# Two token chunks take the first inner half in two parts, with four attention jobs in flight

## The chip, the cores and the metric

The kernel runs on one core of one Trainium2 chip. The metric is the device time of one execution in microseconds (us); lower is better. The kernel before takes 661.24 us in the median of three runs (659.5 to 663.07). Engine names are those of the profile: PE (TensorE matmuls), DVE (VectorE), ACT (ScalarE), POOL (GpSimd), SP (the engine that issues the DMAs).

## The reference

Three layers follow each other: an attention, a gated two-layer network, and a mixture of four experts. Weights, queries, keys and values arrive in float32, except that the network's weights `w_in` and `w_out` are float64 in memory.

```
q, k, v: 2 batches x 8 heads x 576 tokens x 64
q_d, k_d, v_d = means over groups of 4 tokens                # 144 tokens
out_d   = softmax(q_d k_d^T / 8) v_d, repeated 4 times
scores  = q k^T / 8, kept where |i - j| < 4
x = out_d + softmax(scores) v                                # 1152 tokens x 512
h = x @ w_in (512 x 2048);  g = h * sigmoid(h);  x = g @ w_out (2048 x 512)
p = domain_probs / sum
out = sum over 4 experts of p[:, e] * (relu(x @ w1[e]) @ w2[e])   # 512 -> 1024 -> 512
```

## The kernel before, in words

**Attention.** A job is one batch, one pair of heads (four pairs) and one token part (256 or 320 tokens): 16 jobs, numbered in the order batch, part, pair. Jobs 0 to 3 give the 256 tokens of chunk 0, jobs 4 to 7 the 320 of chunk 1, and so on. Each job has named steps, which the orders below use with the job's number: S (local scores on PE), x (maximum and subtraction on DVE), e (exponential on ACT), q, k, p (sums of four queries or keys), D (scores of the averaged tokens on PE), n and d (their maximum on DVE, exponential on ACT), u and r (sums, reciprocals and scaling on DVE), g (scaling on ACT), T (transposes on PE), a (copies on ACT), v (sums of four values on POOL), V (values on PE), o, f (the two attentions added), h and l (x split into a high and a low part, on ACT and DVE). A tail per batch (tp, tD, nt, dt, ...) does the averaged queries of the last 64 tokens.

**Network.** Every float32 product is done as three products of split operands (`mm3`, L563 to L567): high x high, high x low, low x high. `w_in` and `w_out` come as eight units of four pieces (512 KB each): units 0 and 1 are the first inner half (1024 of 2048) of `w_in`, units 2 and 3 that half of `w_out`, units 4 to 7 the second half. A piece s is loaded and split: A (one or two ACT passes over the raw float64), B (one DVE pass, for the pieces in `LOW_ON_DVE`), C (DVE, L230), w (high part), L (low part, POOL, L240). `G c_f_k` is one row block of the first product (chunk c, inner block f of 8, quarter k of the 512 inputs), `H c_d_f` one block of the second (output block d of 4, inner block f). After the G of a block come th (tanh on ACT), gf (DVE, L586), gh (ACT) and gl (DVE, L592). `M k` is G of chunk 0 for the first three inner blocks, quarter k, taken while attention runs; it needs only job k's part of x and piece k.

**Order in time.** For each inner half, the chunks follow one another: all eight G blocks of a chunk, then its H, so chunk 0 needs all 16 pieces of units 0 to 3 before chunk 1 begins. PSUM has three `mm` tiles for these products, two `s` tiles for scores. Work is issued with a priority by tick; `WRITTEN` (L861) then fixes, for each engine apart, the order of the named steps of jobs 0 to 7, chunk 0 and the G of chunk 1. Jobs 8 to 15 are placed by ticks, beside chunk 1's H and chunk 2's G. From chunk 2's H on, and in the experts (L794), there is no attention left.

```
    for hf in range(2):
        u0 = 4 * hf
        for ci, (o, n) in enumerate(CHUNKS[hf]):
            for ft in range(8):
                    g1_step(u0, ft, o, n)
            for db in range(4):
                    g2_step(u0 + 2, hf, [db], o, n)
```

Of the kernel before, what the change touches and what calls it, by code (L numbers as in the profile page):

```python
# [57 lines left out]
LOW_ON_DVE = (0, 3, 9, 13)  # L58
WHI_ON_DVE = (3, 4)
# [4 lines left out]
def attention_moe_kernel(ctx, tc, kqa, kqb, qtl, va, vb, w64, w1d, w2d, dpr, out):  # L64
# [136 lines left out]

    def split_piece():
        u, j, t = loaded.popleft()
        i = 4 * u + j
# [3 lines left out]
        if i < 10 or 11 < i < 15 or i > 15:  # L208
            load_piece()

    def split_raw(u, j, t):
        if j == 0:
            unit[u] = slot(u)
        h, l = unit[u]
        if u < 8:
            c = slice(j * 512, (j + 1) * 512)
# [10 lines left out]
            else:  # L227
                low = mark(f"A{4 * u + j}", ACT.activation(out=v[:, :, 0], in_=top, func=ACTF.Copy, scale=2.0 ** -13,  # L228
# [4 lines left out]
            if 4 * u + j == 16:  # L233
                for a, b in ((first, "gh0_7"), (low, "gh0_7"), (i, "gl0_7")):
                    follow(a, steps[b][-1], "written order")
            if 4 * u + j in WHI_ON_DVE:
                mark(f"w{4 * u + j}", DVE.tensor_copy(out=h[:, c], in_=d))
            else:
                mark(f"w{4 * u + j}", ACT.activation(out=h[:, c], in_=d, func=ACTF.Copy))  # L239
            mark(f"L{4 * u + j}", POOL.tensor_tensor(out=l[:, c], in0=d, in1=h[:, c].bitcast(F32), op=ALU.subtract))  # L240
        else:
            c = slice(j * 1024, (j + 1) * 1024)
# [6 lines left out]
    a2 = actx.enter_context(tc.tile_pool(name="a2", bufs=2))  # L249
    a4 = actx.enter_context(tc.tile_pool(name="a4", bufs=4))  # L250
# [9 lines left out]

    def constants():
        POOL.memset(mask, 0.0)
        for h in range(2):
            m = mask[64 * h:64 * h + 64]
            POOL.affine_select(out=m, in_=m, pattern=[[0, 6], [1, WIN]], compare_op=ALU.is_ge,
                               fill=NEG, base=0, channel_multiplier=-1)
            POOL.affine_select(out=m, in_=m, pattern=[[0, 6], [-1, WIN]], compare_op=ALU.is_ge,
                               fill=NEG, base=6, channel_multiplier=1)
        POOL.memset(mask[:, 0, 0:3], NEG)
        POOL.memset(mask[:, 5, WIN - 3:WIN], NEG)  # L270
        make_identity(nc, ident)
# [13 lines left out]
    def load_kq(j):  # L285
        kw = S + 6 if j.c == 0 else CT[1] + 6
        if j.i == 3:
            j.kq = acc[:, 0:kw + j.n]
# [4 lines left out]
        i = load(f"kq{j.i}", j.kq, (kqa, kqb)[j.c][j.b, j.hp])  # L293
        if j.i == 3:
            first_kq.append(i)
        elif j.i in (4, 5):
            follow(i, first_kq[0], "first jobs")
        elif j.i in (8, 9):
            follow(i, piece_load[j.i + 5], "weights")
# [12 lines left out]
    def load_vg(j):  # L312
        if j.c == 0:
# [4 lines left out]
            i = load(f"vg{j.i}", j.vg, va[j.b, j.hp, :, 0:1024])  # L318
            if j.i == 8:
                follow(i, piece_load[13], "weights")  # L320

    def load_tail(l):
        t = ac.tile([128, 256, 4], F32, tag="vg", name="qt")
        l.t = t[:, 0:64]
        i = load("qt" if l.b == 0 else "qt1", l.t, qtl[l.b].rearrange('p (n r) -> p n r', r=4))
        if l.b == 0:
            follow(i, first_kq[0], "first jobs")
# [23 lines left out]
    def pool_kq_first(j):  # L351
        kd[j.b, j.hp] = a4.tile([128, SD], F32, tag="kd", name="kd")
        k4 = j.k[:, 3:3 + S].rearrange("p (n r) -> p n r", r=4)
        mark(f"k{j.i}", DVE.tensor_reduce(out=kd[j.b, j.hp], in_=k4, axis=AX.X, op=ALU.add))
        j.qd = qbd[j.hp % 2]
        q4 = j.q[:, 0:256].rearrange("p (n r) -> p n r", r=4)
        for h in range(2):
            p = slice(64 * h, 64 * h + 64)
            mark(f"q{j.i}", DVE.tensor_reduce(out=j.qd[p, h], in_=q4[p], axis=AX.X, op=ALU.add))
# [55 lines left out]
    def down_scores(j):  # L415
        i = PE.matmul(out=j.ps[:, 352:352 + SD], lhsT=j.qd.rearrange("p a b -> p (a b)"), rhs=kd[j.b, j.hp],
# [19 lines left out]
    def norm(j):  # L436
# [4 lines left out]
        if nb:  # L441
            j.sm = a2.tile([128, nb, WIN], F32, tag="sm", name="sm")
# [69 lines left out]
    def plan_jobs():  # L512
        k = 0
        for b in range(NB):
            for c in range(2):
                for hp in range(HP):
# [46 lines left out]
    def mm3(ps, pairs, first, last):  # L563
# [534 lines left out]
```

## Time and profile before

| what | value |
|---|---|
| median of three runs | 661.24 us (659.5 to 663.07) |
| span of the profiled execution, first to last instruction | 657.7 us |
| median less that span (what lies around it, and the spread of runs) | 3.5 us |
| PE busy in the span | 630.2 us (96%) |
| DVE, ACT, POOL busy | 418.8, 327.6, 245.3 us |

The profile states no other time for the profiled execution than its span. Busy times of one engine are joined where instructions overlap; a single instruction's duration overlaps its neighbour's by about 0.1 us on DVE and ACT, so sums below use the distance between starts. The idle time of PE lies almost wholly in the first 76 us and in the last 18 us; in between PE is busy without a break.

### The profile page before, as it was taken

What the parts mean: (1) busy time and instruction counts of PE and PEld (TensorE: products, weight loads), DVE (VectorE), ACT (ScalarE), POOL (GpSimd) and SP (SyncE); (2) the same over time, 40 slices, a digit from 0 to 9 for tenths busy, and PEclk for the clock granted to TensorE, in tenths of its full rate; (3) what the DMA queues carried; (4) which work ended last, traced back from release to release, by engine and by line L of the source; (5) the groups of instructions that cost most, each with busy time, mean ns of one, the idle gap of its engine ahead of it and who ended that gap; (6) DMA issues with size and microseconds to landing.
All of it is one profiled execution on the core that took longest, in us unless ns stands there. A gap on an engine that the chain in (4) does not pass through costs nothing.

```text
span 657.7 us, 13693 instructions
## 1 busy us (share of the span) xinstructions
PE 630.2 (96%) x5484; PEld 616.3 (94%) x5484; DVE 418.8 (64%) x862; ACT 327.6 (50%) x744; POOL 245.3 (37%) x345
## 2 busy tenths in 40 slices
PE   4788999999999999999999999999999999999995
PEld 3677899999999999999999999999999999999995
DVE  6698465655545545766558956668954679755434
ACT  4789654568845434363345633346533356433321
POOL 5554651114510001653456322645522564333210
PEclk9899999999999999999999999999999999999998
DMA  9986512106612200240004310014300020000001
GB/s 260 328 283 181 170 54 73 26 5 196 191 59 65 65 1 1 65 161 1 1 1 129 97 33 2 1 34 129 97 1 1 1 65 1 1 33 33 1 33 50
DMA packets 16928, 48.17 MB, mean 73 GB/s; under 512 B 2976, under 2 KB 4256, under 8 KB 16864
## 3 DMA queue, kind: packets, MB, share of 16 engines
q1 hardware_dynamic: 16864, 47.29, 23.4%
q8 instruction: 43, 0.70, 0.5%
q14 instruction: 21, 0.17, 0.1%
HBM read 44.93 MB, written 2.36 MB: 72 GB/s over the span
## 4 chain that ended last, share of the span: by engine, by line
PE 79%; DMA 11%; DVE 3%; ACT 3%; POOL 2%; issue 1%; SPq 0%; ACTq 0%; POOLq 0%; DVEq 0%
PE mm L565 50%; PE p L794 26%; DMA stg<-in_w_dram 4%; DMA vg<-in_va_dram 2%; DMA acc<-in_kqa_dram 2%; DMA acc<-in_w_dram 2%; DMA qt<-in_qtl_dram 1%; DVE dec L230 1%; ACT stg L228 1%; PE t L455 1%; POOL vg L330 1%; ACT dec L222 1%; DMA kq<-in_kqa_dram 1%; PE o L487 1%; DVE acc L822 1%
## 5 line engine op out<-in xcount | busy, mean ns | idle before, releaser
L565 PE MATMUL mm<-xh,wbuf 128*128 128x256 f32 (+2 forms) x1280 | 263.8, 293 | 2.6 <-DVE gf L586 2.3
L565 PEld LDWEIGHTS mm<-xh,wbuf 128*128 128x128 f32 x1280 | 208.2, 188 | 4.1 <-DVE gf L586 3.3
L565 PE MATMUL mm<-xl,wbuf 128*128 128x256 f32 (+2 forms) x640 | 186.9, 292 | 0.0
L776 POOL TENSOR_TENSOR r<-r 128x128 f32<-128x128 f32 x160 | 95.3, 608 | 177.6 <-ACT r L770 136.2
L779 DVE TENSOR_TENSOR h<-r,h 128x384 fp32r<-128x384 f32 (+1 forms) x128 | 91.9, 719 | 64.5 <-ACT h L778 64.2
L778 ACT ACTIVATE h<-r 128x384 fp32r<-128x384 f32 (+1 forms) x128 | 73.7, 578 | 93.7 <-POOL r L776 54.2
L565 PEld LDWEIGHTS mm<-xl,wbuf 128*128 128x128 f32 x640 | 120.3, 188 | 0.0
L565 PE MATMUL mm<-gh,wbuf 128*128 128x256 f32 (+2 forms) x512 | 103.3, 295 | 0.3 <-DVE gf L586 0.2
L794 PE MATMUL p<-wext,h 128*128 128x256 f32 x672 | 89.4, 276 | 0.0
L565 PEld LDWEIGHTS mm<-gh,wbuf 128*128 128x128 f32 x512 | 82.2, 188 | 1.2 <-ACT acc L635 0.4
L794 PE MATMUL p<-wbuf,h 128*128 128x256 f32 x672 | 82.7, 276 | 0.0
L794 PEld LDWEIGHTS p<-wext,h 128*128 128x128 f32 x672 | 82.4, 188 | 0.0
L794 PEld LDWEIGHTS p<-wbuf,h 128*128 128x128 f32 x672 | 79.4, 188 | 0.0
L565 PE MATMUL mm<-gl,wbuf 128*128 128x256 f32 (+2 forms) x256 | 74.1, 292 | 0.0
L776 DVE TENSOR_TENSOR r<-r 128x128 f32<-128x128 f32 x96 | 39.3, 409 | 35.6 <-ACT r L770 31.2
L770 ACT ACTIVATE r<-mm 128x512 f32<-128x512 f32 x48 | 28.6, 597 | 65.3 <-PE mm L565 65.0
L565 PEld LDWEIGHTS mm<-gl,wbuf 128*128 128x128 f32 x256 | 48.1, 188 | 0.1
L592 DVE TENSOR_TENSOR gl<-gf,gh 128x256 fp32r<-128x256 f32 (+2 forms) x64 | 34.6, 543 | 17.9 <-ACT gh L591 17.5
L240 POOL TENSOR_TENSOR wbuf<-dec,wbuf 128x512 fp32r<-128x512 f32 x24 | 32.0, 1350 | 33.8 <-ACT wbuf L239 32.3
L591 ACT ACTIVATE gh<-gf 128x256 fp32r<-128x256 f32 (+2 forms) x64 | 28.1, 442 | 21.6 <-DVE gf L586 20.7
L822 DVE SCALAR_TENSOR_TENSOR acc<-p,pr,acc 128x256 f32<-128x256 f32 (+1 forms) x63 | 36.1, 604 | 3.5 <-PE p L794 3.0
L586 DVE SCALAR_TENSOR_TENSOR gf<-th,mm 128x256 f32<-128x256 f32 (+2 forms) x64 | 28.5, 451 | 14.9 <-ACT th L585 13.9
(138 smaller groups left out, 895.8 us busy)
## 6 DMA issues: line engine op xcount, KB each, us to landing
stg<-in_w_dram SPq DMA_DIRECT2D x25, 512.0 KB
kst<-in_w2d_dram SPq DMA_DIRECT2D x16, 512.0 KB
kst<-in_w1d_dram SPq DMA_DIRECT2D x12, 512.0 KB
acc<-in_w_dram SPq DMA_DIRECT2D x7, 512.0 KB
kq<-in_kqb_dram SPq DMA_DIRECT2D x8, 323.0 KB
kq<-in_kqa_dram SPq DMA_DIRECT2D x6, 419.0 KB
stg<-in_w1d_dram SPq DMA_DIRECT2D x4, 512.0 KB
vw<-in_vb_dram SPq DMA_DIRECT2D x8, 180.0 KB
```

The lines of the kernel that those rows point to most:

```text
L222: first = ACT.activation(out=d, in_=v[:, :, 1].bitcast(F32), func=ACTF.Prelu, scale=2.0 ** -112, alpha=2.0 ** 32)
L240: mark(f"L{4 * u + j}", POOL.tensor_tensor(out=l[:, c], in0=d, in1=h[:, c].bitcast(F32), op=ALU.subtract))
L565: ins = [PE.matmul(out=ps, lhsT=l, rhs=r, start=(first and i == 0), stop=(last and i == n - 1)) for i, (l, r) in enumerate(pairs)]
L586: mark(f"gf{c}_{ft}", DVE.scalar_tensor_tensor(out=gf[:, 0:n], in0=th[:, 0:n], scalar=1.0, in1=ps[:, 0:n], op0=ALU.add, op1=ALU.mult))
L591: latest[ACT] = mark(f"gh{c}_{ft}", ACT.activation(out=gh[ft][:, 0:n], in_=gf[:, 0:n], func=ACTF.Copy))
L592: latest[DVE] = mark(f"gl{c}_{ft}", DVE.tensor_tensor(out=gl[ft][:, 0:n], in0=gf[:, 0:n], in1=gh[ft][:, 0:n].bitcast(F32), op=ALU.subtract))
L770: ACT.activation(out=r[:, 0:4].rearrange("p s t -> p (s t)"), in_=ps[:, 0:512], func=ACTF.Relu)
L776: latest[eng] = eng.tensor_tensor(out=r[:, o], in0=r[:, a], in1=r[:, b], op=op)
L778: ACT.activation(out=h, in_=r[:, part], func=ACTF.Copy)
L779: latest[DVE] = DVE.tensor_tensor(out=l, in0=r[:, part], in1=h.bitcast(F32), op=ALU.subtract)
L794: ins = [PE.matmul(out=ps, lhsT=x, rhs=y, start=(opens and k == 0 and i == 0), stop=(k == 3 and i == n - 1), skip_group_check=True) for i, ...
L822: DVE.scalar_tensor_tensor(out=o, in0=ps, scalar=p, in1=o, op0=ALU.mult, op1=ALU.add)
```

## The change

Chunks 0 and 1 take the first inner half in two parts: `quarter(ci, p, ...)` does four G blocks and the half of H that belongs to them, for chunk 0 part 0, chunk 1 part 0, chunk 0 part 1, chunk 1 part 1. Part 0 needs only units 0 and 2, part 1 units 1 and 3, and the pieces are loaded and split in the order of units 0, 2, 1, 3. The sum of the first part waits in `acc`, and the second is added to it by a DVE instruction. `M` covers all four blocks of chunk 0 part 0, in two PSUM tiles with two blocks each. Jobs 0 to 3 have their scores open at once: jobs 2 and 3 in two of the `mm` tiles. Their averaged keys move from DVE to POOL; jobs 0 and 1 don't use them for D but sum over the raw keys on PE. The written order now covers all 16 jobs and chunks 0 and 1 whole, up to the first product of chunk 2. The second inner half and the experts are as before.

```diff
         u0 = 4 * hf
+        if hf == 0:
+            for p in range(2):
+                for ci in range(2):
+                    main_at[1] = ci
+                    quarter(ci, p, *CHUNKS[0][ci])
...
+            if hf == 0 and ci < 2:
+                continue
...
+    def quarter(ci, p, o, n):
+        c = slice(o, o + n)
+        g = [4 * ci + i for i in range(4)]
+        two = n == 256
+        for i in range(4):
+            next_step()
+            ft = 4 * p + i
+            if (ci, p) == (0, 0):
+                g1_evac(half(hold[i // 2], i % 2), ft, n, g[i])
+            else:
+                g1_step(0, ft, o, n, g[i])
+            attn_tick()
+        flush()
+        if two:
+            b = [mm_tile() for _ in range(2)]
+            groups = [[(d, half(b[d // 2], d % 2)) for d in range(4)]]
+        else:
+            groups = [[(d, mm_tile()) for d in ds] for ds in ((0, 1, 2), (3,))]
...
+                        m = PE.matmul(out=ps[:, 0:n], lhsT=a[:, s], rhs=y, start=(not z and i == 0 and x == 0),
+                                      stop=(i == 3 and x == 2), skip_group_check=True)
...
+                if p == 0:
+                    i = ACT.activation(out=ya, in_=ps[:, 0:n], func=ACTF.Copy, scale=0.5)
+                else:
+                    i = DVE.scalar_tensor_tensor(out=ya, in0=ps[:, 0:n], scalar=0.5, in1=ya, op0=ALU.mult, op1=ALU.add)
...
-LOW_ON_DVE = (0, 3, 9, 13)
-WHI_ON_DVE = (3, 4)
+LOW_ON_DVE = (0, 1, 2, 3)
+WHI_ON_DVE = ()
+RAW_D = (0, 1)
...
+    ORDER = (0, 2, 1, 3)
+    firsts = deque((u, j) for u in ORDER for j in range(4))
...
-    def pool_kq_first(j):
...
-        mark(f"k{j.i}", DVE.tensor_reduce(out=kd[j.b, j.hp], in_=k4, axis=AX.X, op=ALU.add))
...
+    def pool_q_first(j):
+        j.qp = a4.tile([128, 64], F32, tag="qp", name="qp")
+        mark(f"q{j.i}", DVE.tensor_reduce(out=j.qp, in_=j.q.rearrange("p (n r) -> p n r", r=4), axis=AX.X, op=ALU.add))
...
+    def pool_k_first(j):
...
+        mark(f"k{j.i}", fold(k4), padd(kd[j.b, j.hp], k4[:, :, 0], k4[:, :, 1]))
...
-        j.ps = s_p.tile([128, 512], F32, tag="s", name="s")
+        j.ps = mm_tile() if j.i in (2, 3) else s_p.tile([128, 512], F32, tag="s", name="s")
...
+        if j.i in RAW_D:
+            k4 = j.k[:, 3:3 + S].rearrange("p (n r) -> p n r", r=4)
+            first = [None, None]
+            for r in range(4):
+                for h in range(2):
+                    p = slice(64 * h, 64 * h + 64)
+                    i = PE.matmul(out=j.ps[p, 352:352 + SD], lhsT=j.qp[p], rhs=k4[p, :, r], start=(r == 0), stop=(r == 3),
+                                  skip_group_check=True)
...
     WRITTEN = (
...
-        """S0 S1 D0 D1 S2 T0 S3 T1 V0 D2 D3 V1 M0 T2 V2 M1 T3 S4 V3 M2 D4 S5 M3 tD G0_3_0 G0_3_1 D5 G0_3_2 G0_3_3
...
+        """S0 S2 S1 D0 S3 D1 D2 T0 S4 D3 V0 T1 S5 D4 V1 T2 M0 D5 T3 V2 tD M1 S6 V3 T4 M2 D6 S7 tT M3 V4 T5 D7 S8 H0_0_0
+        H0_1_0 H0_2_0 H0_3_0 T6 V5 H0_2_1 H0_0_1 H0_1_1 D8 S9 G1_0_0 H0_3_1 H0_2_2 H0_3_2 H0_0_2 H0_1_2 T7 V6 G1_0_1 S10
...
```

On PE, at the end of chunk 0's early blocks: rows of before from the last three matmuls of M3 on. `o` and `t` are PSUM tiles of V and T, `s` of S and D.

```order
L565 MATMUL mm<-xh,wbuf 128x256 x2
L565 MATMUL mm<-xl,wbuf 128x256
L565 MATMUL mm<-xh,wbuf 128x256
L424 MATMUL s<-kd,qdl 32x144 x4
L565 MATMUL mm<-xh,wbuf 128x256
L565 MATMUL mm<-xl,wbuf 128x256
L565 MATMUL mm<-xh,wbuf 128x256 x2
L565 MATMUL mm<-xl,wbuf 128x256
L565 MATMUL mm<-xh,wbuf 128x256
L416 MATMUL s<-kd,qbd_103 128x144
```

After M3 come more G blocks of chunk 0, and a D. The same place of the changed kernel, where L981 is M and L696 is H:

```order
L981 MATMUL mm<-xl,wbuf 128x256
L981 MATMUL mm<-xh,wbuf 128x256
L514 MATMUL o<-atd_618,vd 64x80 x4
L518 MATMUL o<-at,vw 64x64 x10
L486 MATMUL t_717<-ident,sm 70x128 x4
L486 MATMUL t_718<-ident,sm 70x128
L488 MATMUL t_718<-ident,ed 72x128 x2
L444 MATMUL s<-kd,qbd_106 128x144
L399 MATMUL s<-kq 64x70 x8
L406 LDWEIGHTS ident_103
L406 MATMUL s<-mask,ident_103 128x280
L696 MATMUL mm<-gh_765,wbuf 128x256
```

M3 is now followed by V4, T5, D7 and S8, four jobs' worth of different steps, and then at once by H.

On POOL, the first work on inputs. `vg_f` are values of the first jobs, `kq`, `kq_f`, `acc` keys and queries, `wbuf` the low part of a weight piece. Before:

```order
L330 TENSOR_TENSOR vg_f_156<-vg_f_156 72x256x2
L330 TENSOR_TENSOR vd<-vg_f_156 72x256
L330 TENSOR_TENSOR vg_f_186<-vg_f_186 72x256x2
L330 TENSOR_TENSOR vd<-vg_f_186 72x256
L240 TENSOR_TENSOR wbuf<-dec,wbuf 128x512 x2
```

Changed:

```order
L341 TENSOR_TENSOR vg_f_147<-vg_f_147 72x256x2
L341 TENSOR_TENSOR vd<-vg_f_147 72x256
L341 TENSOR_TENSOR acc<-acc 128x144x2
L341 TENSOR_TENSOR kd<-acc 128x144
L341 TENSOR_TENSOR kq<-kq 128x144x2
L341 TENSOR_TENSOR kd<-kq 128x144
L292 MEMSET qbd_105 128x128
L292 MEMSET qbd_106 128x128
L341 TENSOR_TENSOR kq<-kq 128x144x2
L341 TENSOR_TENSOR kd<-kq 128x144
L341 TENSOR_TENSOR kq<-kq 128x64x2
```

Four pairs of key sums (k2 stands just ahead of these rows) now stand in POOL's queue, three of them between the first v and the first L.

## Rows read from the trace of the kernel before

**Rows 1.** Stretches: length, busy us (instructions) per engine, PE clock, DMA share, GB/s

```profile
4.20:20.00 15.80, 10.55 (x108) 7.92 (x108) 13.85 (x35) 7.11 (x17) 7.44 (x10) 1.00 1.01 282
20.00:40.00 20.00, 14.28 (x184) 12.00 (x179) 14.98 (x42) 17.12 (x43) 11.78 (x18) 0.91 0.96 328
40.00:60.00 20.00, 16.94 (x201) 15.12 (x200) 19.24 (x47) 18.62 (x53) 10.48 (x12) 1.00 0.72 206
60.00:75.80 15.80, 15.03 (x181) 13.68 (x180) 8.22 (x18) 11.90 (x29) 10.76 (x16) 1.00 0.61 191
75.80:128.40 52.60, 52.35 (x565) 48.22 (x563) 30.55 (x91) 28.11 (x85) 15.30 (x32) 1.00 0.24 66
128.40:150.20 21.80, 21.80 (x229) 21.34 (x229) 13.24 (x30) 13.44 (x36) 5.08 (x4) 1.00 0.17 42
```

The engines stand in the order PE, PEld (weight loads), DVE, ACT, POOL.

**Rows 2.** What PE waited for: us in total, times, longest us

```profile
PE s L389 <- DMA kq<-in_kqa_dram: 4.2, 1, 4.2
PE s L389 <- DVE s L439: 3.6, 1, 3.6
PE mm L565 <- DVE gf L586: 2.5, 5, 1.0
```

**Rows 3.** Chain that ended last, two pieces: start us, us, what

```profile
98.44 4.69 PE mm L565 x32
136.40 3.88 PE mm L565 x34
```

**Rows 4.** PE's timeline: start us, us, line, operation, tiles, shape, count

```profile
4.16 1.20 PE L389 MATMUL s<-kq 64*64 64x70 f32 x16 [4.16 <-DMA kq<-in_kqa_dram]
...
69.50 0.71 PE L389 MATMUL s<-kq 64*64 64x70 f32 x16
...
70.37 0.71 PE L389 MATMUL s<-kq 64*64 64x70 f32 x16
...
75.82 0.30 PE L565 MATMUL mm<-xh,wbuf 128*128 128x320 f32 x1
...
150.20 0.30 PE L565 MATMUL mm<-xh,wbuf 128*128 128x320 f32 x1
```

**Rows 5.** DVE's timeline, columns as in the group before

```profile
5.07 0.75 DVE L354 TENSOR_REDUCE kd<-kq 128x144 f32<-128x576 f32 x1
...
46.40 0.17 DVE L439 TENSOR_SCALAR s<-s 128x6 f32<-128x6 f32 x1
...
47.27 0.68 DVE L230 SCALAR_TENSOR_TENSOR dec<-dec,acc 128x512 int32<-128x512 int32 x1
47.87 1.50 DVE L592 TENSOR_TENSOR gl<-gf,gh 128x256 fp32r<-128x256 f32 x1
49.40 0.42 DVE L586 SCALAR_TENSOR_TENSOR gf<-th,mm 128x256 f32<-128x256 f32 x1
49.74 0.52 DVE L404 TENSOR_REDUCE st<-s 128x5 f32<-128x350 f32 x1
...
50.73 0.51 DVE L404 TENSOR_REDUCE st<-s 128x5 f32<-128x350 f32 x1
```

**Rows 6.** DVE by line and shape, 0 to 150 us: busy us, mean ns

```profile
L230 DVE SCALAR_TENSOR_TENSOR dec<-dec,stg 128x512 int32<-128x512 int32 x14 | 10.1, 728 | 3.9 <-ACT dec L222 3.6 <-issue 0.2
L592 DVE TENSOR_TENSOR gl<-gf,gh 128x256 fp32r<-128x256 f32 x16 | 9.1, 578 | 1.2 <-ACT gh L591 1.0
```

**Rows 7.** POOL by line and shape, 0 to 150 us

```profile
L240 POOL TENSOR_TENSOR wbuf<-dec,wbuf 128x512 fp32r<-128x512 f32 x16 | 21.3, 1344 | 22.2 <-ACT wbuf L239 20.7 <-DVE wbuf L237 1.5
...
L330 POOL TENSOR_TENSOR vg_f<-vg_f 72x512 f32<-72x512 f32 x4 | 4.1, 1036 | 6.3 <-DMA vg_f<-in_va_dram 6.3
...
L330 POOL TENSOR_TENSOR kq<-kq 128x288 f32<-128x288 f32 x4 | 2.9, 728 | 0.2 <-PE s L389 0.2
L330 POOL TENSOR_TENSOR vd<-vg_f 72x256 f32<-72x256 f32 x4 | 2.6, 647 | 0.3
L330 POOL TENSOR_TENSOR kd<-kq 128x144 f32<-128x144 f32 x4 | 2.5, 628 | 0.0
```

**Rows 8.** POOL's timeline, the instruction beside the long gl of Rows 5

```profile
47.34 1.74 POOL L240 TENSOR_TENSOR wbuf<-dec,wbuf 128x512 fp32r<-128x512 f32 x1 [3.11 <-ACT wbuf L239]
```

More of the change, by code (lines that the diff above doesn't have):

```diff
@@ L232, in split_raw @@
             mark(f"C{4 * u + j}", i)
-            if 4 * u + j == 16:
-                for a, b in ((first, "gh0_7"), (low, "gh0_7"), (i, "gl0_7")):
-                    follow(a, steps[b][-1], "written order")
             if 4 * u + j in WHI_ON_DVE:
-                mark(f"w{4 * u + j}", DVE.tensor_copy(out=h[:, c], in_=d))
+                mark(f"w{4 * u + j}", DVE.tensor_copy(out=h, in_=d))
             else:
-                mark(f"w{4 * u + j}", ACT.activation(out=h[:, c], in_=d, func=ACTF.Copy))
-            mark(f"L{4 * u + j}", POOL.tensor_tensor(out=l[:, c], in0=d, in1=h[:, c].bitcast(F32), op=ALU.subtract))
-        else:
+                mark(f"w{4 * u + j}", ACT.activation(out=h, in_=d, func=ACTF.Copy))
+            mark(f"L{4 * u + j}", POOL.tensor_tensor(out=l, in0=d, in1=h.bitcast(F32), op=ALU.subtract))
+        else:
+            if j == 0:
+                unit[u] = slot(u)
+            t2, o = unit[u]
+            h, l = t2[:, o:o + UW], t2[:, o + UW:o + 2 * UW]
             c = slice(j * 1024, (j + 1) * 1024)
@@ L287, in load_kq @@
         if j.i == 3:
-            j.kq = acc[:, 0:kw + j.n]
+            j.kq = acc[:, 0:838]
         elif j.i == 2:
@@ L292, in load_kq @@
             j.kq = a2.tile([128, kw + j.n], F32, tag=f"kq{j.c}", name="kq")
[L293 to L299, printed above, removed]
+        load(f"kq{j.i}", j.kq, (kqa, kqb)[j.c][j.b, j.hp])
         j.k, j.q = j.kq[:, :kw], j.kq[:, kw:]
@@ L317, in load_vg @@
                 j.vg = ac.tile([128, 256, 4], F32, tag="vg", name="vg")[0:72]
-            i = load(f"vg{j.i}", j.vg, va[j.b, j.hp, :, 0:1024])
-            if j.i == 8:
-                follow(i, piece_load[13], "weights")
+            load(f"vg{j.i}", j.vg, va[j.b, j.hp, :, 0:1024])
     def load_tail(l):
@@ L324, in load_tail @@
         l.t = t[:, 0:64]
-        i = load("qt" if l.b == 0 else "qt1", l.t, qtl[l.b].rearrange('p (n r) -> p n r', r=4))
-        if l.b == 0:
-            follow(i, first_kq[0], "first jobs")
+        load("qt" if l.b == 0 else "qt1", l.t, qtl[l.b].rearrange('p (n r) -> p n r', r=4))
     def padd(o, a, b):
@@ L415, in down_scores @@
     def down_scores(j):
+        if j.i in RAW_D:
[6 more added lines that the diff above has]
+                                  skip_group_check=True)
+                    after(i, j.group)
+                    mark(f"D{j.i}", i)
+            return
+        if j.i < 4:
+            for h in range(2):
+                p = slice(64 * h, 64 * h + 64)
+                i = PE.matmul(out=j.ps[p, 352:352 + SD], lhsT=j.qp[p], rhs=kd[j.b, j.hp][p], start=True, stop=True)
+                after(i, j.group)
+                mark(f"D{j.i}", i)
+            return
         i = PE.matmul(out=j.ps[:, 352:352 + SD], lhsT=j.qd.rearrange("p a b -> p (a b)"), rhs=kd[j.b, j.hp],
@@ L892, in start_mm @@
     def start_mm(hp):
-        for i in range(HOLD):
-            if hp == 0:
-                hold.append(mm_tile())
-            mark(f"M{hp}", *mm3(hold[i][:, 0:256], g1_pairs(0, i, hp, slice(0, 256)), hp == 0, hp == HP - 1))
+        if hp == 0:
+            hold.extend(mm_tile() for _ in range(2))
+        for i in range(4):
+            ps = half(hold[i // 2], i % 2)
+            for x, (l, r) in enumerate(g1_pairs(0, i, hp, slice(0, 256))):
+                m = PE.matmul(out=ps, lhsT=l, rhs=r, start=(i % 2 == 0 and hp == 0 and x == 0), stop=(hp == HP - 1 and x == 2),
+                              skip_group_check=True)
+                if hp == 0 and x == 0:
+                    if i % 2:
+                        after(m, opened)
+                    else:
+                        opened = m
+                mark(f"M{hp}", m)
     main_parts.append(start_mm)
```

261 lines of the change are left out of this document (147 added, 114 removed).

## The prediction

> **What bounds the kernel now.** I read the table of stretches first, then PE's waits, then the timelines. The table says where PE loses time: 5.25 us idle of 15.80 up to 20 us, 5.72 of 20 up to 40, 3.06 of 20 up to 60, 0.77 of 15.80 up to 75.8, and after that 0.25 in 52.6 and nothing in 21.8 [rows 1]. With the 4.2 us to the first keys [rows 2] that is 19.2 us. In those stretches DVE is busy 48.1 of 55.8 us (86%), and from 40 to 60 DVE is at 96% and ACT at 93% [rows 1]: PE waits because two engines that work through their lists in order are full. PE's waits agree: after the first keys the longest is for DVE, 3.6 us, and the most frequent is for gf on DVE, five times, 2.5 us [rows 2].
>
> Idle is not all. **What PE has to do** can be summed. One matmul of 256 columns takes 3.88/34 = 0.114 us, one of 320 columns 4.69/32 = 0.147 us [rows 3]. A chunk of the first half has 192 of them: 21.9 us for chunk 0 or 2, 28.1 us for chunk 1. Chunk 1 begins at 75.82 and chunk 2 has ended at 150.20 [rows 4]: 74.4 us less 0.25 idle, of which the two chunks are 50.0. The other 24.1 us, with two score blocks that ran already at 69.5 (0.87 us each, the distance of their starts [rows 4]), are eight attention jobs and a tail: 3.2 us a job. So chunks 0 and 1 and 16 jobs are 50.0 + 51.7 = 101.7 us of PE work. The changed kernel does exactly this before chunk 2 begins. Before, the same work, taken as everything up to 150.2 less chunk 2's 21.9, is done at 128.3: 26.6 us are lost, 19.4 idle and some 7 in slow early matmuls (sixteen score matmuls take 1.20 us at the start and 0.71 later [rows 4]; from 20 to 40 us the granted clock is 0.91 [rows 1]). The gain is 128.3 less the time at which the changed kernel reaches chunk 2.
>
> **The change part by part.** Nothing of the network's PE work goes or comes. D of jobs 0 and 1 by raw keys adds 14 matmul calls and D of jobs 2 and 3 two; they stand where PE waits anyway, and only lengthen the first latency.
>
> The main effect is on what has to be ready before PE can run freely. Before, that point is 75.8: jobs 0 to 7, all 16 pieces and eight blocks of chunk 0. After, it is l7, the last part of x for chunk 1: jobs 0 to 7, ten pieces (units 0 and 2, s4, s5) and four blocks. Until then PE can do only what the written order puts ahead: 8 jobs 25.6, S8 to S10 2.6, D8 to D10 and T8 some 1.2, M and H of the first part 96 x 0.114 = 10.9, and 18 matmuls of chunk 1, 2.6. Together 42.9 us.
>
> DVE sets l7. Before, its busy time up to 75.8 is 13.85 + 14.98 + 19.24 + 8.22 = 56.3 us [rows 1]. By the distances of starts, r costs 0.87, C 0.60, gf 0.34 (with gl an unhindered 0.42) and x 0.99 [rows 5]. Off the list go: six C, 3.6; four key reductions, 4 x 0.75 = 3.0 [rows 5]; gf and gl of four blocks, 4 x 0.76 = 3.0; two casts of w, 0.8, now on ACT; half of the query sums, 1.7, as one instruction now covers both heads. Added are x10, u8, r8, n8, n9: 0.99 + 0.5 + 0.87 + 0.8 = 3.2. That leaves 47.4 us, from 4.2 on. At 96% (the stretch 40 to 60) l7 is at 53.6; at the 80.5% of 4.2 to 40 (28.83 of 35.8 us) at 63.1. I take 88%, close to the 86% of the whole and a little over it, since with four jobs open a list has more that is ready: 53.9 us, l7 at 58.1. ACT loses more than DVE (six pieces with three passes, four blocks with two) and takes the two w; by its own sum it ends ahead of DVE. PE has then lost 58.1 - 42.9 = 15.2 us, against 26.6.
>
> The key sums that leave DVE cost POOL four pairs of 0.73 + 0.63 us, 5.4 us [rows 7]. Queued on POOL behind them are v1 and the first L, and M0 waits for that L. POOL's whole list up to the last split of unit 2 (L11: eight L of 1.34, six key pairs, five v of 1.7, eight small sums) is some 36 us from 4.9 on, so 41 if it never waits. H of the fourth block, V7 and o7, f7, h7, l7 come behind it, about 4 us: 45 against 58, so 13 us for its waits are covered by DVE. Without that cover each us would be on the path.
>
> On SP's queue kq4 and kq5 move ahead of most weights, and unit 1's pieces behind unit 2's. The first 26 transfers up to s11, 9.5 MB by their sizes, are done at about 33 us at the 282 and 328 GB/s of rows 1, ahead of POOL's L11. Units 1 and 3 come later than before, but G of the second part stands some 20 us of PE work behind l7, and POOL has 15 us of work up to the last L of unit 1: hidden. The ACT table load now waits for x0 and is 1.3 us on the first chain; e0 came at 7.6 before and should come at about 8, since x0 no longer stands behind k0 and q1 on DVE.
>
> Then the rest: 101.7 - 42.9 = 58.8 us of PE work. DVE has some 41 us for it (70%): its 100.1 us busy up to 150.2, less chunk 2's blocks, the pieces of unit 4 and the shares, less the 47.4 done, plus eight additions into acc at 0.45 like gf. ACT has about 44 (75%). Bounds for PE's stalls: 0.25 of 52.6 (0.5%: 0.3 us, DVE at 58%) and 3.06 of 20 (15%: 9 us, DVE at 96%) [rows 1]. Nearest is 60 to 75.8, ACT at 75%: 0.77 of 15.8, 4.9%. I take 3 us. Chunk 2 begins at 58.1 + 58.8 + 3 = 119.9, and the gain is 128.3 - 119.9 = 8.4 us. Everything behind is PE without gaps and moves as a whole; the pieces of units 4 to 7 get more time, not less. The profiled span goes from 657.7 to 649.3, the median, 3.5 us above the span, to 652.8.
>
> [...] The gl at 47.87 took 1.50 us instead of 0.42, beside a low-part subtraction of POOL from 47.34, 1.74 us long [rows 5, 8]; the mean of 16 gl is 578 ns, so 0.16 us extra each, and C has a mean of 728 ns over its 680 [rows 6]. [...]
>
> **Rivals.** (1) Clean: DVE keeps 96% and PE hardly stalls: 53.6 + 58.8 + 0.3 = 112.7, a gain of 15.6, 645.6 us. For it: four jobs open cover latencies. Against it: no stretch with an empty start reached it. (2) Given back: l7 at 63.1 and stalls up to 15%: 124.9 to 130.9, between a gain of 3.4 and a loss of 2.6; middle 661. For it: every engine runs in one written order, and one late step holds all behind it. (3) Slower: PSUM hand-over. Three mm tiles serve 24 groups between M and chunk 2, and jobs 2 and 3 hold two of them at the start; each tile comes back only behind attention steps in the lists of DVE and ACT, and eight of them by the new additions on DVE. The longest such wait of before is 1.0 us [rows 2]. From 128.3 - 58.1 - 58.8 = 11.4 us over 24, that is 0.48 us a hand-over, nothing is left; at 0.8 us it is 19.2, and 669. Against it: 20 like hand-overs from 75.8 to 150.2 cost 0.25 us in all [rows 1]. [...] That the weights of the second part are late is covered by 20 us and gets no chance of its own.
>
> **How the numbers follow.** Forecast 0.60 (own range 648 to 657), clean 0.10, given back 0.18, hand-over 0.08, lock 0.04. What a measurement of this kernel tells from no change is about 0.5%, 3.3 us: faster is below 657.9, slower above 664.5. Faster: forecast and clean, and a third of given back, 0.76. Same: most of the rest of it, 0.11. Slower: 0.13. The range reaches from the clean case, 644.5, to just past the middle of given back, 662.
>
> **What would show it.** Right: l7 (the last DVE L531 before the first long run of 320-column matmuls) at 54 to 62 us; the first chunk 2 matmul near 120; PE idle up to there near 15 us instead of 19; DVE near 88% busy until l7; the experts' part as long as before. Wrong: PE's waits for gf or the new additions adding up to over 8 us after 60 us (hand-over); gl and C with means near 1 us (lock); POOL as the releaser of H (the POOL list is the bound); or a longer second half.

## The result and the profile after

The changed kernel took 654.83 us (the profiled execution, span 653.1) and 652.66 us, a ratio to the kernel before of 0.989 (0.984 to 0.994). Two more executions of that set took 664.69 and 663.42 us, as long as the kernel before, at a granted clock of 0.998; lying over 1.5% above the fastest they count as slow and are not in the ratio, and as none of them was profiled, their cause is open. Measured again later in six executions on another chip, it took 651.09 us in the median (649.98 to 652.32) against 662.88 for the kernel before there, a ratio of 0.9835 (0.9805 to 0.9866). So it is faster by 1.1 to 1.65%, 7 to 11 us; forecast were 652.8 us and a gain of 8.4.

The stretches of [rows 1], in the profiled execution after (stretch, its length, busy time and instructions of PE, PEld, DVE, ACT and POOL, granted clock, DMA share, GB/s):

```profile
4.20:20.00 15.80, 13.48 (x164) 9.95 (x163) 11.59 (x34) 8.33 (x22) 10.74 (x20) 1.00 0.95 274
20.00:40.00 20.00, 17.66 (x221) 14.91 (x219) 17.20 (x48) 15.18 (x45) 12.96 (x21) 0.91 0.87 270
40.00:60.00 20.00, 19.64 (x264) 17.63 (x263) 18.09 (x45) 18.20 (x53) 14.46 (x21) 1.00 0.63 187
60.00:75.80 15.80, 15.80 (x174) 14.55 (x174) 13.07 (x36) 13.93 (x38) 11.78 (x16) 1.00 0.63 201
75.80:100.00 24.20, 24.01 (x286) 22.32 (x287) 16.80 (x46) 19.48 (x57) 12.59 (x19) 1.00 0.48 155
100.00:128.40 28.40, 26.84 (x261) 25.01 (x260) 18.08 (x43) 16.21 (x43) 5.35 (x5) 1.00 0.27 74
128.40:150.20 21.80, 20.56 (x166) 20.00 (x166) 9.25 (x17) 14.63 (x33) 5.41 (x5) 1.00 0.51 162
```

PE's idle time up to 75.8 us falls from 19.2 to about 9 us: 2.32 + 2.34 + 0.36 + 0 behind the first 4. Behind 100 us there is more of it than before, where there was almost none. PE's waits (total, times, longest), against [rows 2]:

```profile
PE s L399 <- DMA kq<-in_kqa_dram: 4.7, 2, 4.0
PE mm L599 <- DVE gf L621: 1.3, 3, 0.5
PE t L486 <- DVE sm L474: 0.9, 1, 0.9
PE s L444 <- ACT s L420: 0.7, 2, 0.6
PE mm L599 <- ACT acc L717: 0.7, 1, 0.7
PE mm L599 <- DVE acc L710: 0.7, 1, 0.7
```

The waits for gf are no longer at the start: two of the three, the one for acc on ACT and the one for acc on DVE stand in chunk 2. PE's timeline (start, duration) has the marks that the rest goes by: S7, the scores of job 7; the first matmuls of chunk 2, of chunk 3 and of the second half:

```profile
37.58 0.83 PE L399 MATMUL s<-kq 64*64 64x70 f32 x20 [0.29 <-DVE st L468]
...
120.36 0.39 PE L599 MATMUL mm<-xh,wbuf 128*128 128x256 f32 x1 [0.68 <-DVE acc L710]
...
144.68 0.30 PE L599 MATMUL mm<-xh,wbuf 128*128 128x320 f32 x1
...
173.88 0.28 PE L599 MATMUL mm<-xh,wext 128*128 128x256 f32 x1
```

Chunk 3 started at 150.20 before [rows 4] and the second half at 180.06. DVE's timeline has l7 at 59.76, and at chunk 2's start the last addition, the four instructions for the shares, and only then the first gf:

```profile
59.76 0.49 DVE L531 TENSOR_TENSOR xl<-o,xh 128x320 fp32r<-128x320 f32 x1
...
121.02 0.48 DVE L710 SCALAR_TENSOR_TENSOR acc<-mm,acc 128x320 f32<-128x320 f32 x1
121.42 0.18 DVE L1012 TENSOR_REDUCE pr<-pr 128x9 f32<-128x36 f32 x1
121.64 0.68 DVE L1014 TENSOR_SCALAR pr<-pr 128x9 f32<-128x9 f32 x1
122.35 0.22 DVE L1015 RECIPROCAL pr<-pr 128x9 f32<-128x9 f32 x1
122.60 0.99 DVE L1016 TENSOR_TENSOR pr<-pr 128x36 f32<-128x36 f32 x1
123.51 0.41 DVE L621 SCALAR_TENSOR_TENSOR gf<-th,mm 128x256 f32<-128x256 f32 x1
```

What stood between the first keys and l7 is read from the chain that ended last (start, us, what). Each piece in it released the next, or was the instruction ahead of it on its engine:

```profile
11.63 0.32 DVE stf L459
...
28.09 0.53 DVE sm L474
...
28.76 0.71 PE s L452 x8
29.46 2.86 PE mm L981 x12
...
33.38 0.54 DVE st L414
...
48.88 1.37 DVE gl L627
...
50.30 1.54 PE mm L696 x11
```

From 11.63 to 28.62 us the chain is DVE's list without a break, and DVE is busy 16.3 of these 17.0 us. Then PE has it up to the scores of job 6. From 33.38 to 50.25 it is DVE's list again, but for S7 and some short issue times; from 50.30 on it is PE's list. In the execution measured again it looks alike: DVE from 10.87 to 28.6 us, steps of a job on ACT, DVE from 30.6 to 47.85 but for S7, then PE.

### The profile page after: what moved, and what is told of

Its sections match the earlier page's. It is cut to its first block, busy times and chain, and to the rows that moved or that the text cites. A ratio compares the mean times of both kernels' runs of the same rounds, so it can differ in the third digit from the quotient of the medians.

```text
span 653.1 us, 13762 instructions
## 1 busy us (share of the span) xinstructions
PE 633.6 (97%) x5516; PEld 618.9 (95%) x5516; DVE 420.1 (64%) x860; ACT 326.1 (50%) x746; POOL 253.0 (39%) x353
## 4 chain that ended last, share of the span: by engine, by line
PE 82%; DVE 8%; DMA 4%; issue 3%; ACT 2%; POOL 1%; SPq 0%; DVEq 0%; ACTq 0%; POOLq 0%
PE mm L599 49%; PE p L874 27%; DMA stg<-in_w_dram 3%; PE mm L696 2%; DVE dec L243 1%; DMA kq<-in_kqa_dram 1%; PE s L399 1%; DVE gf L621 1%; DVE gl L627 1%; PE o L518 1%; DVE acc L902 1%; DVE sm L474 1%; DVE o L523 1%; POOL wbuf L250 0%; ACT gh L626 0%
## 5 line engine op out<-in xcount | busy, mean ns | idle before, releaser
L599 PE MATMUL mm<-xh,wbuf 128*128 128x256 f32 (+2 forms) x1248 | 258.5, 293 | 1.3 <-DVE acc L710 0.7
L599 PEld LDWEIGHTS mm<-xh,wbuf 128*128 128x128 f32 x1248 | 203.1, 188 | 2.8 <-DVE acc L710 0.9
L599 PE MATMUL mm<-xl,wbuf 128*128 128x256 f32 (+2 forms) x624 | 181.9, 292 | 0.0
L599 PEld LDWEIGHTS mm<-xl,wbuf 128*128 128x128 f32 x624 | 117.2, 188 | 0.0
L599 PE MATMUL mm<-gh,wbuf 128*128 128x256 f32 (+2 forms) x384 | 76.1, 294 | 1.7 <-DVE gf L621 1.0
L599 PEld LDWEIGHTS mm<-gh,wbuf 128*128 128x128 f32 x384 | 61.6, 188 | 2.3 <-DVE gf L621 1.4
L853 ACT ACTIVATE r<-mm 128x512 f32<-128x512 f32 x48 | 28.6, 597 | 65.3 <-PE mm L599 65.0
L599 PE MATMUL mm<-gl,wbuf 128*128 128x256 f32 (+2 forms) x192 | 55.5, 294 | 0.0
L627 DVE TENSOR_TENSOR gl<-gf,gh 128x256 fp32r<-128x256 f32 (+2 forms) x64 | 38.0, 595 | 16.0 <-ACT gh L626 15.8
L802 POOL TENSOR_TENSOR wext<-kst,wext 128x512 fp32r<-128x512 f32 x8 | 10.4, 1302 | 78.9 <-ACT wext L800 43.1
```

The costliest lines, as they stand in the source:

```text
L599: ins = [PE.matmul(out=ps, lhsT=l, rhs=r, start=(first and i == 0), stop=(last and i == n - 1)) for i, (l, r) in enumerate(pairs)]
L627: latest[DVE] = mark(f"gl{c}_{ft}", DVE.tensor_tensor(out=gl[g][:, 0:n], in0=gf[:, 0:n], in1=gh[g][:, 0:n].bitcast(F32), op=ALU.subtract))
L853: ACT.activation(out=r[:, 0:4].rearrange("p s t -> p (s t)"), in_=ps[:, 0:512], func=ACTF.Relu)
```

## The experiments

All edits are to the changed kernel. The marks of the profiled executions, and the medians, in us (the runs came in three sets on three chips; ratios are to the kernel before on the same chip):

| kernel | S7 | l7 | l7 - S7 | chunk 3 | second half | median | ratio |
|---|---|---|---|---|---|---|---|
| changed, first profile | 37.58 | 59.76 | 22.18 | 144.68 | 173.88 | | 0.989 |
| changed, again | 35.18 | 57.34 | 22.16 | 142.99 | 171.84 | 651.09 | 0.9835 (0.9805-0.9866) |
| key sums on DVE | 37.65 | 59.81 | 22.16 | 145.12 | 173.78 | 654.43 | 0.9903 (0.9874-0.9931) |
| more on POOL | 39.45 | 61.63 | 22.18 | 147.83 | 176.51 | 653.61 | 0.9896 (0.9866-0.9925) |
| more on PE | 41.48 | 65.25 | 23.77 | 150.27 | 178.77 | 654.38 | 0.9903 (0.9870-0.9937) |
| two jobs open | 49.13 | 71.32 | 22.19 | 157.66 | 186.84 | 667.52 | 1.0102 (1.0071-1.0133) |
| two jobs open, b | 48.78 | 70.96 | 22.18 | 155.98 | 184.31 | 667.54 | 1.0080 (1.0053-1.0107) |
| short order | 38.28 | 62.67 | 24.39 | 151.27 | 179.43 | 657.56 | 0.9936 (0.9908-0.9963) |
| short order, by chunk | 38.92 | 63.47 | 24.55 | 160.20 | 188.36 | 668.30 | 1.0108 (1.0067-1.0149) |
| additions early | 35.21 | 57.39 | 22.18 | 140.94 | 169.68 | 651.11 | 0.9841 (0.9809-0.9873) |
| additions early, splits held | 37.28 | 59.46 | 22.18 | 139.96 | 170.95 | 651.76 | 0.9851 (0.9814-0.9887) |
| D by sums | 35.46 | 57.61 | 22.15 | 142.25 | 170.40 | 652.30 | 0.9873 (0.9832-0.9914) |
| D by sums, additions early | 35.34 | 57.85 | 22.51 | 142.09 | 172.39 | 653.50 | 0.9875 (0.9829-0.9921) |

The two profiles of the changed kernel itself have S7 2.4 us apart. A smaller difference in S7 or l7 between two profiles tells nothing by itself; what tells is the path that led there.

**Which engine sets l7?** First DVE gets the key sums back.

```
-        mark(f"k{j.i}", fold(k4), padd(kd[j.b, j.hp], k4[:, :, 0], k4[:, :, 1]))
+        mark(f"k{j.i}", DVE.tensor_reduce(out=kd[j.b, j.hp], in_=k4, axis=AX.X, op=ALU.add))
...
-        "q0 x0 q1 q2 x1 x2 cz n0 q3 B0 u0 r0 x3 n1 ... n3 x4 ..."
+        "q0 x0 q1 q2 x1 x2 cz k2 n0 q3 B0 u0 r0 x3 k3 n1 ... n3 k0 x4 k1 ..."
```

> The sums of the keys of jobs 0 to 3 go back from POOL to DVE. Theory (DVE's list sets l7): DVE gets 4 x 0.75 = 3.0 us more before l7, which moves from 59.8 to about 63, and the time from about 653.5 to 656 to 657. Rival (POOL's list is the bound): POOL has 5.4 us less to do and the time falls by 2 us or more. Rival (only the order of the parts counts): no change within 1 us.

Four reductions of 0.74 to 0.75 us came onto DVE, and l7 stayed at 59.81. That looks as if DVE's list did not matter, but the path says otherwise. All four stand ahead of f0 in DVE's list; h0 and e4 on ACT follow f0, and D4 on PE follows e4. PE at D4 and at the scores of job 6, in the first profile and then here:

```profile
21.97 0.48 PE L444 MATMUL s<-kd,qbd 128*128 128x144 f32 x2 [0.61 <-POOL wbuf L250]
...
32.25 0.83 PE L399 MATMUL s<-kq 64*64 64x70 f32 x20
```

```profile
23.45 0.48 PE L444 MATMUL s<-kd,qbd 128*128 128x144 f32 x2 [1.93 <-ACT s L420]
...
32.30 0.83 PE L399 MATMUL s<-kq 64*64 64x70 f32 x20
```

D4 came 1.5 us later, and M1 still 1.3 us later. Then the first profile lost as much in another way: it ran M1 at a granted clock of 0.50, 2.86 us instead of 1.58, and DVE waited 1.50 us for the scores behind it. So the equal S7 and l7 are a coincidence. The changed kernel's other profile, in which M1 was not slow, has S7 2.5 us earlier than this run, and the ratios (0.9903 against 0.9835, on two chips) point to a cost as well. The run therefore does not refute that DVE's list sets the start. It does not settle it either, because POOL was 5.4 us lighter at the same time, and beside it three B passes on DVE took 0.59 us on average instead of 0.85.

More on POOL: the second addition of each key sum is issued three times.

```
-        mark(f"k{j.i}", fold(k4), padd(kd[j.b, j.hp], k4[:, :, 0], k4[:, :, 1]))
+        mark(f"k{j.i}", fold(k4), *(padd(kd[j.b, j.hp], k4[:, :, 0], k4[:, :, 1]) for _ in range(3)))
```

> Each of the four key sums of jobs 0 to 3 on POOL writes its second addition three times, 8 x 0.63 = 5.0 us more on POOL ahead of v0 and the first low part. Theory (DVE sets l7, POOL is covered): l7 within 1.5 us of 59.8 and the time up by 0 to 1.5 us. Rival (POOL's list is the bound): l7 and the time up by 4 to 5 us.

l7 came 1.8 us later than with the key sums on DVE in the same set, not 5, and 1.9 and 4.3 us later than in the two profiles of the changed kernel: PE waited 1.3 us for vd and 1.2 us for qbd, both on POOL, at 22 to 25 us. In the median (653.61) no cost shows beside the key sums on DVE. POOL's cover is real but thinner than the 13 us forecast, at this one place.

More on PE, between S7 and l7:

```
-        j.group = PE.matmul(out=j.ps[:, 0:nb * WIN], lhsT=ident16, ...)
+        for _ in range(21 if j.i == 8 else 1):
+            j.group = PE.matmul(out=j.ps[:, 0:nb * WIN], lhsT=ident16, ...)
```

> The mask matmul of job 8, which PE runs at about 43 us, is issued 21 times instead of once: 20 x 0.12 = 2.4 us more of PE work between S7 and l7, none on another engine. Theory (from the scores of job 7 at 37.6 us on, PE's own list sets l7: in four kernels l7 came 22.16 to 22.19 us behind them): l7 and the start of chunk 2 come 2.4 us later, the time is 655 to 656.5. Rival (DVE's list sets l7, PE has room): l7 and the time unchanged within 0.7 us.

Its PE timeline, S7 and the added matmuls:

```profile
41.48 0.83 PE L399 MATMUL s<-kq 64*64 64x70 f32 x20
...
46.90 2.68 PE L407 MATMUL s<-mask,ident 128*128 128x280 bf16 x21
```

One such matmul takes 0.29, so 2.39 us were added, and l7 came 23.77 instead of 22.18 us behind S7: 1.6 of it arrived, the rest fell into the small waits that PE had there, above all the one at 50.30 for a gl on DVE (0.36 us). So between S7 and l7 PE's list and DVE's are nearly equally long: in the first profile PE is busy 21.8 of the 22.2 us and DVE 19.7, and DVE's leads up to that gl by less than 0.8 us. More work on DVE or POOL behind S7 was not tried; what the two runs before added stood ahead of it. (S7 itself is late in this one execution, by a single wait of 4.65 us, while ACT waited 4.80 us for the transfer of a weight piece; the median is 654.38.)

**What sets S7, and what are the three parts worth?** Two jobs open: jobs 2 and 3 start behind the transposes of jobs 0 and 1 on PE, DVE and ACT, and one constant moves ahead on POOL; PE's list shows it.

```
-        "S0 S2 S1 D0 S3 D1 D2 T0 S4 D3 V0 T1 S5 D4 V1 T2 M0 D5 ..."
+        "S0 S1 D0 D1 T0 S2 T1 S3 V0 D2 S4 V1 D3 T2 M0 S5 D4 D5 ..."
```

> Only two attention jobs are open at the start: in the written lists the scores of jobs 2 and 3 stand behind the transposes of jobs 0 and 1, the rest is as in the changed kernel. Theory (four open jobs cover latencies of DVE's list): DVE is busy about 80% instead of 84% up to l7, l7 comes 3 to 5 us later, the time is 656 to 659. Rival (the parts of the chunks bring all of the gain): the same time within 1 us.

667.52: far from both, and slower than the kernel before. DVE had the same 46.6 us of work up to l7, but over 67.1 us, so it was busy 69% instead of 84%. Its PE timeline shows a wait of 4.88 us for v1, and what came behind it; under it the stretch behind the wait:

```profile
25.65 0.70 PE L514 MATMUL o<-atd,vd 72*64 72x64 f32 x8 [4.88 <-POOL vd L341]
...
31.28 0.41 PE L981 MATMUL mm<-xl,wbuf 128*128 128x256 f32 x1
31.49 0.63 PE L981 MATMUL mm<-xh,wbuf 128*128 128x256 f32 x2
...
33.76 1.43 PE L399 MATMUL s<-kq 64*64 64x70 f32 x20
```

```profile
25.60:34.00 8.40, 6.67 (x50) 5.34 (x52) 3.73 (x12) 2.04 (x7) 2.85 (x3) 0.50 0.76 257
```

Behind the wait the granted clock is 0.50: a matmul of 256 columns starts every 0.21 us instead of 0.114 [rows 3], and twenty score matmuls take 1.43 us instead of 0.83. That the wait itself lowered the clock was not shown. Since that wait was POOL's order, a second kernel took it away:

```
-        "... in_s0 in_s1 in_kq4 in_vw0 in_vg1 in_kq5 ..."
+        "... in_s0 in_vg1 in_s1 in_vw0 in_kq4 in_kq5 ..."
-        "cm cb ci k2 v0 k3 k0 cq k1 p4 v1 L0 ..."
+        "cm cb ci v0 k2 v1 L0 k3 k0 cq k1 p4 ..."
```

> Two jobs open at the start as before, but without the wait of 4.9 us that the first such kernel had for the value sums of job 1: they and the first low part stand ahead of the key sums of job 3 on POOL, and their loads ahead of those of job 4. Theory (two open jobs leave PE waiting on the chain of softmax through DVE and ACT): job 7's scores at 42 to 45 us instead of 37.6, the time 657 to 661. Rival (the loss of the first such kernel was POOL's order): job 7's scores within 1.5 us of 37.6, the time 653 to 655.

The wait for v1 is gone and S7 is still at 48.78. Waits of 1.84, 0.95, 0.72 and 2.21 us on the softmax chain through ACT and DVE stand in both kernels; what took the place of the wait for v1 is slower matmuls. From 4.2 us to S7 PE is idle 9.2 us instead of 13.2, but busy 35.3 instead of 31.8, at a granted clock of 0.73 instead of 0.81 (0.59 from 20 to 40 us). Up to 38 us the chain that ended last passes in turn through PE, ACT, DVE and, in the first kernel, POOL, where with four open jobs it lay on DVE for 17 us on end.

Beside the kernels of the same two sets that keep four jobs open, these two are 13 to 16 us slower: with them neither the parts nor the rest of the order gain anything. Both hold job 2 back behind T0, though, while the kernel before has "S0 S1 D0 D1 S2 T0"; an order between two and four open jobs was not tried.

The written order cut behind the eighth job (five lists end at vw7, V7, h7, l7 and L11):

> The written order ends with the eighth job: vw7, V7, h7, l7 and the last split of unit 2. What stands behind is ordered by the scheduler from its priorities. Theory (behind job 7's scores PE has work enough, and the order there decides little): up to S7 as in the changed kernel, then PE idle 1 to 3 us more before chunk 2, the time 653 to 657. Rival (the written order behind job 7 carries the gain): 660 or more.

657.56, just above what the theory allowed: 6.5 us behind the changed kernel in the same set. Three places in its profile hold most of it: l7 comes 2.2 us later behind S7 with PE busy; 10 us behind l7 a V waits 2.2 us for the l of the job ahead of it; and there are 2.1 us for gf in chunk 2. The clock is 0.94 in the stretch of each wait. On top of this short order, chunk 0 takes both parts first (PE's written list then also ends without G1_0_0 and G1_0_1):

```
-            for p in range(2):
-                for ci in range(2):
+            for ci in range(2):
+                for p in range(2):
...
-    ... (1, (-6, -3, 0, 3)), (3, (4, 6, 8, 10))):
+    ... (1, (-8, -7, -6, -5)), (3, (-4, -3, -2, -1))):
```

> The same short written order, and chunk 0 takes both parts of the inner half before chunk 1 takes the first (so units 1 and 3 are split ahead of chunk 1). To be compared with the run that has the short order alone. Theory (PE keeps going from job 7's scores on because the first ten pieces are enough for two chunks; with units 1 and 3 due at once ACT, 92% busy from 40 to 60 us, has 8 pieces of some 2 us more): PE waits for splits between 55 and 80 us, chunk 2 and the time 5 to 10 us later. Rival (the four open jobs alone carry the gain): within 1.5 us of the run with the short order.

10.7 us slower than with the short order alone, so with this order the parts are worth about that. The stretches from 60 to 100 us, first by chunk, then the short order alone:

```profile
60.00:75.80 15.80, 12.22 (x134) 10.00 (x131) 10.02 (x24) 12.72 (x33) 9.89 (x11) 0.78 0.68 205
75.80:100.00 24.20, 19.66 (x207) 17.78 (x206) 15.92 (x44) 16.52 (x47) 10.77 (x18) 0.93 0.55 177
```

```profile
60.00:75.80 15.80, 13.61 (x146) 11.81 (x146) 14.25 (x32) 13.32 (x35) 11.64 (x16) 0.94 0.62 184
75.80:100.00 24.20, 24.00 (x265) 22.04 (x264) 17.15 (x49) 20.45 (x56) 10.72 (x15) 0.97 0.58 183
```

The place is as expected, the releaser only partly. PE's waits by chunk, 40 to 100 us:

```profile
PE o L514 <- DVE xl L531: 2.4, 1, 2.4
PE s L444 <- ACT s L420: 1.5, 1, 1.5
PE o L518 <- ACT at L489: 1.5, 1, 1.5
PE s L444 <- POOL qbd L341: 1.3, 1, 1.3
PE mm L696 <- POOL wbuf L250: 1.0, 1, 1.0
```

Only about 1.5 us is for split weights themselves (two smaller rows have 0.3 and 0.2 us); most is for attention steps on ACT, DVE and POOL. That those stand behind the eight splits in the lists is likely, and was not tried apart. The costs of these experiments do not add up to the gain: each took one part out of an order that was written for all of them.

**What is given back in chunk 2?** First the last additions alone go ahead in DVE's list:

```
-        "... l14 ya1_1_1 f15 ya1_3_1 ya1_0_1 l15 ya1_2_1"
+        "... l14 ya1_1_1 ya1_2_1 ya1_0_1 f15 l15 ya1_3_1"
```

> Only the order of the last additions into acc on DVE is changed: they stand ahead of f15. Theory (chunk 2's first matmul waits 0.68 us for such an addition): chunk 2 starts 0.7 us earlier, at 119.7, and the waits for gf behind it stay; the time falls by 0.7 us, 652.5 to 653.5. Rival (the wait moves on to the next thing): no change.

Then also the splits of units 4 and 5 and the shares wait for the last block of chunk 2's first product:

```
+            if u in (4, 5):
+                behind(ACT, first)
+                behind(DVE, i)
...
         follow(i, last_x[-1], "shares")
+        behind(DVE, i)
```

> Two changes around chunk 2: the additions into acc stand in DVE's list as their sums come ready, ahead of f15, and the splits of units 4 and 5 and the shares stand behind the last block of chunk 2's first product on ACT and DVE. Theory (chunk 2 gives back 0.7 us at its start and 1.6 us in waits for gf and acc beside those splits): the first expert matmul comes 2.3 us earlier, the time is about 651. Rival (the splits are then late for the second half, or wait beside chunk 3 instead): 653 to 655, with waits for gf in chunk 3.

PE's waits from 105 to 143 us with the additions early, and from 139 to 172 us with the splits held as well:

```profile
PE mm L599 <- ACT acc L717: 0.8, 1, 0.8
PE mm L696 <- DVE gf L621: 0.5, 1, 0.5
```

```profile
PE mm L602 <- DVE gf L624: 1.6, 2, 1.2
PE mm L602 <- ACT acc L720: 0.2, 1, 0.2
```

With the additions early the waits for acc on DVE and for gf at chunk 2 are gone, and the way from S7 to chunk 3 is 105.7 instead of 107.1 and 107.8 us. Holding the splits makes it 102.7, but chunk 3 then takes 30.99 instead of 28.74 us, with 1.8 us of waits beside the splits: the rival is right for most of it. In the medians (651.11 and 651.76, on two chips) neither can be told from the changed kernel.

D of jobs 0 and 1 from the key sums (RAW_D empty, POOL's list beginning with "cm cb k0 k1 ci k2 v0 k3 cq"):

> D of jobs 0 and 1 is taken from the key sums, as for jobs 2 and 3, and POOL takes the key sums in the order of the jobs. 12 matmul calls fewer, 2.30 + 2.24 us of slow PE work at 9 to 15 us become about 2 x 0.4. Theory (PE's work and latency up to job 7's scores set the rest): if the four key sums on POOL (1.4 us each, from 5.4 us) come in time, job 7's scores and the time come 1 to 3 us earlier. Rival (the sums are late: the first chain waits for POOL): the same or up to 2 us later.

S7 at 35.46 and 652.30 us: no difference that the spread of S7 among like kernels (35.2 to 37.6) would not cover. With the additions early too, and beside the changed kernel itself:

> The changed kernel with both edits that looked better in their own runs: the last additions into acc ahead of f15, and D of jobs 0 and 1 from the key sums. Theory (each takes time off PE's path: 1.4 us at chunk 2, and up to 2 us before job 7's scores): 649.5 to 651.5. Rival (the difference of the second was only the spread of early transfers): 651 to 652, as with the first edit alone.

> The changed kernel itself, beside the three others of this set. From its two runs so far 652.7 and 654.8; by the theory that early transfers and the pace of one stretch spread the runs, 649 to 655 with a median near 653, and a gain over the kernel before of 7 to 8 us.

653.50 against 651.09: the two edits together gain nothing, so no version here beats the changed kernel. The kernel itself came out below the 653 expected of it, with a gain of 11.8 us in the medians instead of 7 to 8.

## Why the prediction came out right, and where its steps failed

**"DVE sets l7" held for most of the way, not up to l7.** l7 was forecast at 58.1 from DVE alone, 47.4 us at 88%. It came at 59.76 and 57.34, with 46.6 and 46.5 us of DVE work at 84% and 88%. The chain that ended last lies on DVE's list from 11.6 to 28.6 us and, but for S7, from 33.4 to 50.25; the last 9.5 us up to l7 are PE's list. From S7 on both lists together give 22.15 to 22.19 us to l7 in nine of the ten profiles that leave them unchanged there, and 22.51 in the tenth. The reason given for the 88%, that four open jobs keep more ready, is borne out: with two open DVE was busy 69%. That DVE's list sets the pace is read from the traces; no run loads DVE alone, so no experiment shows it.

**PE's loss was used in two meanings.** "PE has then lost 15.2" is l7 less 42.9 us of PE work, like the 26.6 of before; by that measure 16.9 and 14.4 came. As a sign it was taken for idle time, near 15 us up to chunk 2, and that was 10.4 and 8.9. The rest is longer PE work at the start. D of jobs 0 and 1 with raw keys takes 2.30 and 2.24 us where D of job 2 takes 0.43; the prediction put this at nothing, as standing where PE waits anyway. And some matmuls still run at half rate, such as M1 in the first profile: 2.86 us instead of 1.58, at a granted clock of 0.50. The forecast of l7 did not use these terms, so they did it no harm.

**The rest** was sized well: from l7 to chunk 2 forecast 61.8, measured 60.6 with 1.4 us idle. Chunk 2 began at 120.36 and 118.09 against 119.9, a gain of 7.9 and 10.2 by the prediction's reference of 128.3.

**"Everything behind moves as a whole" failed.** Chunk 2's matmuls are 21.9 us of work; from its start to chunk 3 it took 24.3 and 24.9 us. (The 128.3 is a sum and no place in the trace: before, chunk 2's first product began at 117.74, mixed with attention.) PE's waits in it are 1.6 and 2.1 us, for gf behind the shares and the splits and for acc; before, the last l, the shares and those splits stood at 143 to 149 us, at the end of chunk 2, and PE was not idle in the 21.8 us ahead of chunk 3 [rows 1]. The gain of the first profile went on from 5.5 us at chunk 3 to 6.2 at the second half, as a wait of 1.0 us for gf that chunk 3 had before fell to 0.4, and 4.6 at the end; the execution measured again kept 7.2, 8.2 and 8.4 of its 10.2. So 2 to 3 us are a cost that the prediction missed, and another 1.5 us in the first profile is a pace of matmuls told of below.

**Covers and rivals.** The key sums on POOL are not wholly hidden: with five more us there PE waited 2.5 us for POOL, though the median shows no cost. D with raw keys cannot be told from D by sums in the time. The hand-over rival falls: the eight additions made PE wait once, 0.68 us. That work on POOL locks DVE out, the case given 0.04 as "lock", no run shows; with each of the four gl and ten C before l7 as late as the long gl [rows 5], 1.50 us instead of 0.42, it would be 15 us. What the first profile shows before l7 is a mean of 0.91 us instead of 0.42 for four gl, 0.78 instead of 0.68 for ten C and 0.74 instead of 0.42 for four B, 4.3 us in all; what made them longer was not tried apart. One of these gl, 1.45 us long at 48.80 beside additions on POOL (47.55 to 49.96), lies on the chain and made PE wait 0.36 us. "Given back" was right in kind, with 2 to 3 us, and not in size. The range begins at 644.5, called the clean case, which by its own sum is 645.6; nothing hangs on that.

## What to carry to other kernels

Follow the chain that ended last before naming what bounds a start. Here DVE was busy only 84 to 88%, yet the chain lay on its list for most of the way from 11 to 50 us. More jobs in flight shortened the start without taking an instruction away, because that list then had something ready at almost every moment. Two profiles that agree at one mark need not agree in the path to it: an added cost and a slow stretch of matmuls came out equal here. Look at the granted clock behind idle PE time at a start: behind the wait of 4.88 us here it was 0.50, and matmuls of 256 columns came every 0.21 us instead of 0.114. When work is moved forward, look at what else begins as soon as it ends: here the shares and the next splits moved onto a stretch that had been free of them.

## What the runs showed of the hardware

Matmuls of 256 columns came at two paces at the same granted clock of 1.00, every 0.118 us in one profile and every 0.113 us in another. From the second half's start to its last chunk the same instructions took, in the first profile and in the one measured again:

```profile
173.88:240.84 66.96, 66.96 (x578) 66.86 (x577) 33.13 (x74) 27.70 (x65) 1.29 (x1) 1.00 0.10 33
```

```profile
171.84:237.32 65.48, 65.48 (x578) 65.38 (x577) 33.15 (x74) 27.67 (x65) 1.29 (x1) 1.00 0.11 34
```

PE is busy throughout and the clock is 1.00 in both, but from about 201 us on a matmul of 256 columns starts every 0.118 us in the first and every 0.113 us in the second: 1.5 us. With the splits held the slower pace held for the whole stretch, 67.84 us. What sets it stays open. Early transfers differ as well: in the first 12 us these two executions moved

```profile
DMA packets 1023, 3.25 MB, mean 271 GB/s; under 512 B 107, under 2 KB 107, under 8 KB 1023
```

```profile
DMA packets 1229, 3.69 MB, mean 308 GB/s; under 512 B 139, under 2 KB 140, under 8 KB 1229
```

and S7 came at 37.58 and 35.18. The third score block starts at 7.73 against 7.10, and each execution has a stretch at a granted clock of 0.50: in the first it is M1, and DVE waits 1.50 us for the scores behind it; in the second it lies at 18.6 to 21.6 us, where DVE had other work and was busy 2.9 of the 3.0 us. The pace and the early transfers together are as large as the edits of the last experiments.
